# The output stage of an attention and max-of-three layer, done on pairs of token tiles by seven block products

## Chip, cores and metric

The kernel runs on one core of a Trainium2 chip. The metric is the device time of one execution in microseconds (us), lower is better.

## The reference

Attention with a learned bias of relative position, and then a layer that takes the maximum of three products, over 2304 tokens of width 512:

```python
scores = scale * q @ k.T + bias                    # 4 x 8 heads, 576 x 576, head width 64
attn   = exp(scores - max) / (sum + 1e-9)
x      = (attn @ v)                                # rearranged to 2304 x 512
h      = max(max(x @ w1, x @ w2), x @ w3)          # w1, w2, w3: 512 x 768
out    = h @ w_out                                 # w_out: 768 x 512, out 2304 x 512
```

The change touches the last line, and the order in which the line above it is worked out.

## The kernel before, in words

A float32 product is done in three TensorE passes: each operand is split into a high part (a cast to the rounded type float32r, on ScalarE) and a low part (operand minus high part, on VectorE or GpSimd), and a product is high x high + high x low + low x high.

**Attention** runs in 72 steps of 9 per pair of heads and batches (`Attention.step`, L382). Beside it, a stream of small jobs (`first`, L904, drawn by `w0.go`) converts the weights from 64-bit words to float32: per 128 x 512 block one ScalarE operation and four VectorE ones (`convert`, L515). For the sets 3 and 2 of w1..w3 GpSimd also makes four sums of blocks (`sum_w`, L554), and both go to DRAM (`w_d`). The six blocks of w_out are converted in the same stream and stored in `wo_d`. A step draws one VectorE job, or two where the step's number in its nine is 1, 3 or 5 (L977).

**The max-of-three stage** (`moe`, L566) has nine sets of weights: three blocks of 256 columns of h, times the three matrices. h is laid out transposed, with tokens along the columns: three blocks x of 384 columns, each for both halves t of the tokens (1152 each). Set 0 is done plainly (`plain`). The other eight, times three x, are 24 groups (`group`, L592): a Strassen-Winograd scheme with seven products p1 to p7 of 128 x 384, each 6 matmuls of 384 columns, out of four blocks of x (b11, b12, b21, b22) and four sums (t1 to t4). Before, every product has a PSUM bank of its own (8 banks, used in turn); p1 and p5 are copied out by ScalarE (m1, m5), the others are added to them by VectorE, GpSimd makes one add of 768 columns (L614), and the results are put into `ht` by a maximum (two VectorE operations of 768 columns, L623 and L624). After the third set of a column block `store` (L630) writes h to DRAM (`h_d`).

The order is written out by hand: `at(n, k, job)` hangs a job on slot k of group n, and `slot()`, called between products, first takes one entry of the list `after` (the maxima and the stores) and then the jobs of that slot. So preparation of x, of weights and the loads of w_out (L779 to L788) and of h (L817 to L823) stand between products in the queues of ScalarE, VectorE, GpSimd and SyncE, and each queue works in order.

**The output stage** (L840 to L861) goes over 18 tiles of 128 tokens. A tile of h (128 x 768) is loaded from `h_d`, cast by ScalarE (L812) and its low part made by VectorE (L815, through L470); then 18 matmuls of 512 columns: six blocks of 128 of the inner dimension, three passes. ScalarE copies the bank out (L860), SyncE stores it. The last tile is done in two halves of 256 columns. Tile k+1 is prepared, and tile k+5 loaded, before the matmuls of tile k are issued.

Of the kernel before, what the change touches and what calls it, by code (L numbers as in the profile page):

```python
# [19 lines left out]
def kernel(  # L20
# [44 lines left out]
    wo_d = dram.tile([DFF, DM], F32, name="wo_d")  # L65
    w_d = dram.tile([2, 2, 128, 1024], F32, name="w_d")
# [448 lines left out]
    def convert(pool, w, out, name):  # L515
# [13 lines left out]
        nc.vector.scalar_tensor_tensor(out=out, in0=high, scalar=signm, in1=t,  # L529
                                       op0=ALU.bitwise_and, op1=ALU.bitwise_or)  # L530
# [35 lines left out]
    def moe(pool, wpool, x0, xa, xb, raw, sr):  # L566
        ht = pool.tile([128, NX, 5, TW], F32, name="ht", bufs=1)
# [4 lines left out]
        def terms(o, w, xn, r, first, last):  # L572
            hi, lo = w
            h, l = xn
            for j in range(2):
                c = slice(r + 128 * j, r + 128 * j + 128)
                nc.tensor.matmul(o, lhsT=hi[:, c], rhs=h[:, j], start=first and j == 0, stop=False)  # L577
                nc.tensor.matmul(o, lhsT=hi[:, c], rhs=l[:, j], start=False, stop=False)  # L578
                nc.tensor.matmul(o, lhsT=lo[:, c], rhs=h[:, j], start=False, stop=last and j == 1)  # L579

        def plain(x, slot):
            for t in range(2):
                for b in range(2):
                    o = bank(f"c{b}{t}_{x}")[:, 0:TW]
                    for d in range(2):
                        n = (("b11", "b12"), ("b21", "b22"))[d][t]
                        terms(o, wf[0], xs[x][n], 256 * (2 * d + b), d == 0, d == 1)
                        if d:
                            nc.scalar.copy(ht[:, x, 3 * b + t], o)
                        slot()  # L590

        def group(s, x, slot):  # L592
            fp, i = divmod(s, 3)
            acc = ht[:, x]
            q = pool.tile([128, 5, TW], F32, tag="q", bufs=1, name=f"q{s}_{x}") if i else acc
            c21, c22, u, c11, c12 = (q[:, n] for n in range(5))
            m1, m5 = (pool.tile([128, TW], F32, tag="m", bufs=2, name=f"m{n}_{s}_{x}") for n in "15")
            mp = pool.tile([128, 2, TW], F32, tag="mp", bufs=2, name=f"mp{s}_{x}")

            def made(p):  # L600
                o = bank(f"{p}_{s}_{x}")[:, 0:TW]
                w, n = PRODUCTS[p]
                terms(o, wf[s], xs[x][n], 256 * w, True, True)
                return o

            nc.scalar.copy(m1, made("p1"))  # L606
            slot()
            nc.scalar.copy(m5, made("p5"))
            slot()
            arith(v, mp[:, 1], made("p6"), m1, ALU.add)  # L610
            slot()
            arith(v, mp[:, 0], made("p7"), mp[:, 1], ALU.add)
            both = bass.AP(tensor=m5.tensor, offset=m5.offset, ap=[list(m5.ap[0]), [0, 2], [1, TW]])
            g.tensor_tensor(out=q[:, 1:3], in0=mp, in1=both, op=ALU.add)  # L614
            slot()
            arith(v, c11, made("p2"), m1, ALU.add)
            slot()
            arith(v, c21, made("p4"), mp[:, 0], ALU.add)
            slot()
            arith(v, c12, made("p3"), u, ALU.add)  # L620
            slot()
            if i:
                after.append(lambda: arith(v, acc[:, 0:2], acc[:, 0:2], q[:, 0:2], ALU.max))  # L623
                after.append(lambda: arith(v, acc[:, 3:5], acc[:, 3:5], q[:, 3:5], ALU.max))  # L624
            if i == 2:
                after.append(lambda: store(fp, x))
# [3 lines left out]
        def store(fp, x):  # L630
            r = slice(TW * x, TW * x + TW)
            for h in range(2):
                nc.sync.dma_start(out=hd[:, 2 * fp + h, :, r], in_=ht[:, x, 3 * h:3 * h + 2])
# [121 lines left out]
        wor = {}  # L755

        def load_wo(f):
            if f % 2 == 0:
                p, tag = ((wpool, "wr1"), (pool, "wr0"), (wpool, "ws"))[f // 2]
                wor["t"] = p.tile([128, 1024], F32, tag=tag, bufs=1, name=f"wor{f}")  # L760
            wor[f] = wor["t"][:, 512 * (f % 2):512 * (f % 2) + 512]
            nc.sync.dma_start(out=wor[f], in_=wo_d[128 * f:128 * f + 128])

        def raise_wo(f):
            if f == 0:
                for c in "hl":
                    wor[c] = pool.tile([128, 1536], F32R, tag=f"w{c}1", bufs=1, name=f"wo{c}")
            if f < 3:
                wo[f] = tuple(wor[c][:, 512 * f:512 * f + 512] for c in "hl")
            else:  # L770
                wo[f] = tuple(xa.tile([128, 512], F32R, tag=f"f0_{2 * (f - 3) + k}", bufs=1, name=f"wo{c}{f}")
                              for k, c in enumerate("hl"))
            nc.scalar.copy(wo[f][0], wor[f])

        def lower_wo(f, k):
            r = slice(256 * k, 256 * k + 256)
            arith(g, wo[f][1][:, r], wor[f][:, r], wo[f][0][:, r])

        for f in range(KFF):  # L779
            at(23, 0 + (f >= 2) + (f >= 4), F(load_wo, f))  # L780
        n = 3 * NSET - 3
        for f, (up, lows) in enumerate((((n, 0), ((n, 1), (n, 1))), ((n, 3), ((n, 4), (n, 4))),
                                        ((n, 4), ((n, 5), (n, 5))),
                                        ((n + 1, 0), ((n + 1, 1), (n + 1, 1))), ((n + 1, 4), ((n + 1, 5), (n + 1, 5))),
                                        ((n + 2, 0), ((n + 2, 1), (n + 2, 1))))):
            at(*up, F(raise_wo, f))
            for k, where in enumerate(lows):
                at(*where, F(lower_wo, f, k))  # L788

        NK = NT // 128  # L790
        per = TW // 128
        hins = {}
        hs = {}

        def home(k, j, dtype):
            name = f"{('hin', 'hh', 'hl')[j]}{k}"
            if k < 2:
                p, tag = xa, (("f0_6", "f0_7", "r0_0"), ("r0_1", "r0_2", "r0_3"))[k][j]
            else:
                p, tag = xb, f"f1_{3 * ((k - 2) % 3) + j}"  # L800
            return p.tile([128, KFF, 128], dtype, tag=tag, bufs=1, name=name)

        def load_h(k):
            q, c = divmod(k, per)
            x, t = divmod(q, 2)
            hins[k] = home(k, 0, F32)
            c0 = TW * x + 128 * c
            nc.sync.dma_start(out=hins[k], in_=hd[:, :, t, c0:c0 + 128])

        def split_hi(k):  # L810
            hs[k] = (home(k, 1, F32R), home(k, 2, F32R))
            nc.scalar.copy(hs[k][0], hins[k])  # L812

        def split_lo(k):
            arith(v, hs[k][1], hins.pop(k), hs[k][0])  # L815

        n = 3 * NSET - 2  # L817
        at(n, 2, F(load_h, 0))
        at(n, 3, F(load_h, 1))
        at(n + 1, 2, F(load_h, 2), F(split_hi, 0))  # L820
        at(n + 1, 3, F(load_h, 3))
        at(n + 1, 4, F(split_lo, 0))
        at(n + 1, 4, F(load_h, 4))  # L823

        order = [(s, x) for s in range(NSET) for x in range(NX)]
        for n, (s, x) in enumerate(order):
            step = [0]

            def slot():
                for f in after[:1]:  # L830
                    after.pop(0)()
                for f in jobs.pop((n, step[0]), ()):
                    f()
                step[0] += 1

            (plain(x, slot) if s == 0 else group(s, x, slot))
        for f in after:
            f()
        assert not jobs, jobs.keys()
        for k in range(NK):  # L840
            if k + 1 < NK:
                split_hi(k + 1)
                split_lo(k + 1)
            if k + 5 < NK:
                load_h(k + 5)
            hh, hl = hs.pop(k)
            x, t = divmod(k // per, 2)
            t0 = HT * t + TW * x + 128 * (k % per)
            ot = xb.tile([128, DM], F32, tag=f"f2_{k % 4}", bufs=1, name=f"ot{k}")
            parts = 1 if k + 1 < NK else 2  # L850
            for y in range(parts):
                r = slice(y * DM // parts, (y + 1) * DM // parts)
                po = bank(f"o{k}_{y}")[:, 0:DM // parts]
                for f in range(KFF):
                    woh, wol = wo[f]
                    nc.tensor.matmul(po, lhsT=hh[:, f], rhs=woh[:, r], start=(f == 0), stop=False)  # L856
                    nc.tensor.matmul(po, lhsT=hh[:, f], rhs=wol[:, r], start=False, stop=False)  # L857
                for f in range(KFF):
# [186 lines left out]
```

## Time and profile before

| | |
|---|---|
| median of three runs | 587.67 us (587.26 to 588.5) |
| the profiled execution | 587.77 us, of which the span is 586.0 us |
| TensorE busy | 575.4 us, 98% |
| VectorE, ScalarE, GpSimd busy | 76%, 59%, 56% |
| TensorE clock granted | 1.0 in all 40 slices |
| stages of the span | to 306.6 attention, to 331.7 set 0, to 506.9 the 24 groups, to 582.4 the output |

The share of busy time is an average over these four stages, and TensorE is at the top in each. What matters is therefore how long TensorE's instructions in a stage take, and which waits would come to lie between them.

### The profile page before, as it was taken

The page shows a single profiled execution, that of the slowest core. Times are in us where ns is not written, and L with a number is a line of the kernel's source. Part 1 is how long each engine was busy: PE and PEld are TensorE (multiplying, and loading weights), DVE is VectorE, ACT ScalarE, POOL GpSimd, SP SyncE. Part 2 cuts the span into 40 slices and gives each one's busy share as a digit, 9 for nine tenths or more (in the row PEclk, how much of TensorE's full clock was granted, in tenths as well). Part 3 has the DMA queues.
Part 4 walks back from the last instruction along what each step waited for, and adds up shares of the span by engine and source line. Part 5 has one row for each costly group of instructions (what it writes and reads, how often), then busy time and mean ns, then how long its engine had stood idle before and what let it go on. Part 6 is the DMA issues. An engine that isn't in the chain of part 4 may idle for free.

```text
span 586.0 us, 12150 instructions
## 1 busy us (share of the span) xinstructions
PE 575.4 (98%) x4368; PEld 459.6 (78%) x4368; DVE 444.7 (76%) x923; ACT 343.0 (59%) x790; POOL 325.3 (56%) x312
## 2 busy tenths in 40 slices
PE   8999999999999999999999999999999999999997
PEld 4456766666676667676659999999999999988886
DVE  7996779798889999788749899997999566722221
ACT  7996897888888878898746633222212213223231
POOL 1866676876857686776630076686776767400000
PEclk9999999999999999999999999999999999999999
DMA  5898705672684349320001412422123121845442
GB/s 164 240 350 288 254 22 159 219 197 88 196 288 129 105 114 309 107 57 22 22 1 37 141 29 69 158 91 73 36 91 109 36 73 55 242 137 173 141 152 72
DMA packets 70381, 76.85 MB, mean 131 GB/s; under 512 B 22832, under 2 KB 50864, under 8 KB 70320
## 3 DMA queue, kind: packets, MB, share of 16 engines
q1 hardware_dynamic: 70176, 75.77, 41.3%
q8 instruction: 35, 0.57, 0.4%
q10 hardware_dynamic: 144, 0.29, 0.2%
q14 instruction: 26, 0.21, 0.1%
HBM read 49.69 MB, written 26.36 MB: 130 GB/s over the span
## 4 chain that ended last, share of the span: by engine, by line
PE 89%; ACT 5%; DVE 3%; issue 2%; DMA 1%; POOL 0%; DVEq 0%; ACTq 0%
PE pv L359 14%; PE tp L324 11%; PE p L577 10%; PE p L578 10%; PE p L579 10%; PE s L263 10%; PE o L856 4%; PE o L859 4%; PE o L857 4%; PE bp L135 3%; PE s L256 2%; PE c L577 1%; PE c L579 1%; PE c L578 1%; ACT hid L117 1%
## 5 line engine op out<-in xcount | busy, mean ns | idle before, releaser
L298 POOL TENSOR_SCALAR e<-e,rc 128x576 f32<-128x576 f32 x144 | 112.3, 793 | 69.2 <-DVE rc L295 48.9
L286 ACT ACTIVATE e<-sn,nm 128x576 f32<-128x576 f32 x144 | 111.3, 774 | 33.1 <-DVE nm L273 32.1
L273 DVE CUSTOM_DVE_ANT_0 sn<-s,bias 128x576 f32<-128x576 f32 x144 | 103.1, 753 | 21.4 <-PE s L263 17.1
L324 PEld LDWEIGHTS tp<-ident,e 128*128 128x128 f32 x576 | 61.6, 141 | 33.2 <-issue 22.5
L324 PE MATMUL tp<-ident,e 128*128 128x128 f32 x576 | 78.8, 280 | 2.0 <-DVE et L407 1.8
L359 PE MATMUL pv<-et,vt 128*64 128x320 f32 (+1 forms) x496 | 75.3, 419 | 0.1
L606 ACT COPY m<-p 128x384 f32<-128x384 f32 x24 | 11.5, 480 | 94.0 <-PE p L579 52.9
L407 DVE COPY et<-tp 128x512 f32<-128x512 f32 (+1 forms) x80 | 49.6, 629 | 21.0 <-PE tp L324 20.7
L470 DVE TENSOR_TENSOR hl<-hin,hh 128x768 fp32r<-128x768 f32 x18 | 18.1, 1008 | 50.2 <-ACT hh L812 50.2
L614 POOL TENSOR_TENSOR q<-mp,m 128x768 f32<-128x768 f32 x18 | 33.8, 1880 | 36.0 <-DVE mp L470 36.0
L359 PEld LDWEIGHTS pv<-et,vt 128*64 128x64 f32 x496 | 30.8, 136 | 25.2 <-issue 11.1
L263 PE MATMUL s<-kh,qh 64*128 64x288 f32 x256 | 48.5, 344 | 1.2 <-ACT bs L155 0.9
L230 POOL TENSOR_TENSOR kl<-kr,kh 128x576 fp32r<-128x576 f32 x16 | 41.1, 2569 | 15.0 <-ACT kh L227 14.6
L470 DVE TENSOR_TENSOR ht<-ht,q 128x768 f32<-128x768 f32 x36 | 45.8, 1310 | 0.0
L470 POOL TENSOR_TENSOR wl<-wr,wh 128x256 fp32r<-128x256 f32 x25 | 23.6, 955 | 38.5 <-ACT wh L647 38.5
L404 ACT COPY et<-tp 128x512 f32<-128x512 f32 (+1 forms) x72 | 39.5, 548 | 7.9 <-PE tp L324 4.8
L860 ACT COPY ot<-o 128x512 f32<-128x512 f32 (+1 forms) x19 | 10.7, 564 | 56.3 <-PE o L859 56.3
L856 PE MATMUL o<-woh,hh 128*128 128x512 f32 (+1 forms) x114 | 43.4, 385 | 0.0
L135 PE MATMUL bp<-hid,w2s 128*32 128x79 f32 (+51 forms) x640 | 41.0, 393 | 2.2 <-DVE hid L114 1.6
L857 PE MATMUL o<-wol,hh 128*128 128x512 f32 (+1 forms) x114 | 43.0, 381 | 0.0
L263 PE MATMUL s<-kl,qh 64*128 64x288 f32 x256 | 41.0, 295 | 0.0
L114 DVE TENSOR_SCALAR hid<-sm,bp 128x528 f32<-128x528 f32 (+17 forms) x108 | 40.3, 450 | 0.0
(177 smaller groups left out, 1502.2 us busy)
## 6 DMA issues: line engine op xcount, KB each, us to landing
bias_d<-bs SPq DMA_DIRECT2D x36, 295.5 KB, 5.6
bias<-bias_d SPq DMA_DIRECT2D x16, 576.0 KB, 6.4
w<-in_moe_w_dram SPq DMA_DIRECT2D x36, 256.0 KB, 3.3
h_d<-ht SPq DMA_DIRECT2D x18, 384.0 KB, 2.7
hin<-h_d SPq DMA_DIRECT2D x18, 384.0 KB, 3.9
qr<-in_qd_dram SPq DMA_DIRECT2D x16, 288.0 KB, 5.3
kr<-in_kd_dram SPq DMA_DIRECT2D x16, 288.0 KB, 5.1
out_dram<-ot SPq DMA_DIRECT2D x17, 256.0 KB, 4.0
```

The costliest lines, as they stand in the source:

```text
L263: nc.tensor.matmul(ss[h][:, x, 0:HALF], lhsT=u[q][p, 128 * t:128 * t + 128], rhs=u[k][p, cols], start=(j == 0), stop=(j == 2))
L273: nc.vector.tensor_tensor_reduce(out=sn.rearrange("p (a b) -> p a b", a=2), in0=st["s"][h][:, :, 0:HALF], in1=bt.rearrange("p (a b) -> p a ...
L286: nc.scalar.activation(st["e"][:, S * h:S * h + S], sn, ACTF.Exp, scale=-1.0, bias=nm, accum_out=st["sm"][:, h:h + 1])
L298: nc.gpsimd.tensor_scalar(out=e, in0=e, scalar1=rc[:, h:h + 1], scalar2=1.0, op0=ALU.mult, op1=ALU.mult)
L324: nc.tensor.transpose(tp[:, 128 * c:128 * c + 128], e2[:, k0:k0 + 128], ident)
L359: nc.tensor.matmul(pv[p], lhsT=w, rhs=x, start=(c == 0), stop=(c == NTQ))
L470: eng.tensor_tensor(out=out, in0=f(a), in1=f(b), op=op)
L577: nc.tensor.matmul(o, lhsT=hi[:, c], rhs=h[:, j], start=first and j == 0, stop=False)
L578: nc.tensor.matmul(o, lhsT=hi[:, c], rhs=l[:, j], start=False, stop=False)
L579: nc.tensor.matmul(o, lhsT=lo[:, c], rhs=h[:, j], start=False, stop=last and j == 1)
L856: nc.tensor.matmul(po, lhsT=hh[:, f], rhs=woh[:, r], start=(f == 0), stop=False)
L857: nc.tensor.matmul(po, lhsT=hh[:, f], rhs=wol[:, r], start=False, stop=False)
```

## The change

Three parts.

1. *The output stage* takes two tiles of 128 tokens at once, one of each half of the tokens, as a product of 2 x 2 blocks: h by token half and by half of the inner dimension (384), w_out by the same and by half of its columns (256). Seven products with K = 384 and 256 columns replace eight: 9 matmuls each, 63 for a pair, 9 pairs. The sums of blocks of w_out are made during attention and read back (`load_wo`, `raise_wo`, `lower_wo`); those of h are made per pair (`h_sum`), followed by casts (`h_high`) and low parts (`h_low`) of the tiles A (two blocks), B (one), C (t1, t3) and D (t2, t4).
2. *Stages in one bank.* In groups and pairs p6, p7 and p4 go on accumulating on p1's bank, and p3 on p5's; ScalarE copies the bank's content out between (u2, u3). GpSimd's add of 768 columns is gone, and the maximum of the other three blocks is one operation of 1152 columns. The order is p5, p6, p2, p7, p1 of the next group, p4, p3. Slots come before the products. The last two pairs are interleaved.
3. *Attention's stream* converts w_out in blocks like the other weights and makes their sums beside the next conversion (`pend`); a step draws two VectorE jobs only at 1 and 3 of its nine.

```diff
-    wo_d = dram.tile([DFF, DM], F32, name="wo_d")
-    w_d = dram.tile([2, 2, 128, 1024], F32, name="w_d")
+    w_d = dram.tile([2 + KFF // 2, 2, 128, 1024], F32, name="w_d")
...
+            def made(p, on=None):
+                o[p] = o[on] if on else bank(f"{p}_{s}_{x}")[:, 0:TW]
                 w, n = PRODUCTS[p]
+                terms(o[p], wf[s], xs[x][n], 256 * w, not on, True, bool(on))
+                return o[p]
+
+            def p1():
+                o["m1"] = keep("m1", 2)
+                nc.scalar.copy(o["m1"], made("p1"))
+            def p5():
+                made("p5")
+                o["q"] = pool.tile([128, 3, TW], F32, tag="q", bufs=1, name=f"q{s}_{x}") if i else acc[:, 1:4]
+            def p6():
+                o["u2"] = keep("u2", 2)
+                nc.scalar.copy(o["u2"], made("p6", "p1"))
+            def p2():
+                arith(v, o["q"][:, 1], made("p2"), o["m1"], ALU.add)
+            def p7():
+                u3 = keep("u3", 1)
+                nc.scalar.copy(u3, made("p7", "p1"))
+                arith(v, o["q"][:, 0], o["p5"], u3, ALU.add)
+            def p4():
+                if i:
+                    arith(v, acc[:, 0], acc[:, 0], made("p4", "p1"), ALU.max)
+                else:
+                    nc.scalar.copy(acc[:, 0], made("p4", "p1"))
+            def p3():
+                arith(v, o["q"][:, 2], made("p3", "p5"), o["u2"], ALU.add)
+                if i:
+                    after.append(lambda: arith(v, acc[:, 1:4], acc[:, 1:4], o["q"], ALU.max))
+                if i == 2:
+                    after.append(lambda: store(fp, x))
...
+        for k, p in enumerate(USE):
+            at(n - 1, k, F(load_wo, p))
+        for p, up, low, eng in (("p1", (n, 0), (n, 2), v), ("p5", (n, 2), (n, 4), v), ("p6", (n + 1, 0), (n + 1, 1), g),
+                                ("p2", (n + 1, 2), (n + 1, 3), g), ("p7", (n + 1, 4), (n + 1, 5), v),
+                                ("p4", (n + 2, 0), (n + 2, 1), g), ("p3", (n + 2, 4), (n + 2, 4), g)):
+            at(*up, F(raise_wo, p))
+            at(*low, F(lower_wo, p, eng))
...
+        n = 3 * NSET
+        for m in range(NP):
+            at(*((n - 2, 3) if m == 0 else (n - 1, 0) if m == 1 else (n + m - 2, 0)), F(load_h, m))
+            w = n + m - 1
+            if m:
+                at(w, 0, F(h_sum, m, "t1", "t3"), F(h_high, m, "A"))
+                at(w, 2, F(h_high, m, "C"), F(h_sum, m, "t2", "t4"))
+            else:
+                at(w - 1, 6, lambda m=m: h_sum(m, "t3", "t1", "t2", "t4", eng=g))
+                at(w, 0, F(h_high, m, "A"))
+                at(w, 3, F(h_high, m, "C"))
+            at(w, 1, F(h_low, m, "A"))
+            at(w, 3, F(h_low, m, "C"))
+            at(w, 4, F(h_high, m, "B"))
+            at(w, 5, F(h_low, m, "B"))
+            at(w, 6, F(h_high, m, "D"), F(h_low, m, "D"))
...
+                for c in range(3):
+                    k, r = slice(128 * c, 128 * c + 128), slice(256 * c, 256 * c + 256)
+                    nc.tensor.matmul(o[p], lhsT=hi[:, k], rhs=wh[:, r], start=not on and c == 0, stop=False, **skip)
+                    nc.tensor.matmul(o[p], lhsT=hi[:, k], rhs=wl[:, r], start=False, stop=False, **skip)
+                    nc.tensor.matmul(o[p], lhsT=lo[:, k], rhs=wh[:, r], start=False, stop=c == 2, **skip)
...
+        groups = [group(s, x) for s in range(1, NSET) for x in range(NX)] + [out_pair(m) for m in range(NP)]
+        groups[0][0]()
+        for n, (_, p5, p6, p2, p7, p4, p3) in enumerate(groups[:-2]):
+            now[:] = [NX + n, 0]
+            for f in (p5, p6, p2, p7, groups[n + 1][0], p4, p3):
+                slot()
+                f()
+        (_, a5, a6, a2, a7, a4, a3), (b1, b5, b6, b2, b7, b4, b3) = groups[-2:]
+        now[:] = [NX + len(groups) - 2, 0]
+        for f in (a5, a6, a2, a7, b1, a4, b6, a3, b7, b5, b4, b2, b3):
+            slot()
+            f()
...
+                for token in convert(wpool, ahead.pop(0), out, name):
+                    yield token
+                    if token == "vector" and pend:
+                        pend.pop(0)()
...
+            parked = [(f"{s}", s - PARK[1]) for s in PARK] + [(f"o{i}", 2 + i) for i in range(KFF // 2)]
+            for name, k in parked:
+                made, half = block(name)
                 for d in range(2):
+                    yield from conv(lambda: half(d), f"{name}_{d}")
+                nc.sync.dma_start(out=w_d[k, 0], in_=made[0])
+                pend.extend(sums(made[0], name, k))
...
-                more += [w0] * (2 if n % NS in (1, 3, 5) else 1)
+                more += [w0] * (2 if n % NS in (1, 3) else 1)
```

In a pair the functions p1 to p3 are as in a group, with 256 columns, no maximum, and p4 copied out by ScalarE; the low parts of h stand on VectorE, the sums of pair 0 on GpSimd. A token tile is stored whole after p4 (first half of the tokens) and after p3 (second half), and in halves for the last pair.

## Rows read from the trace of the kernel before

**Rows 1.** Busy time by stage: stretch, length, busy us (instructions) of each engine, clock, DMA

```profile
306.56:331.65 25.09, 25.09 (x146) 25.09 (x145) 22.00 (x26) 17.15 (x28) 0.00 (x0) 1.00 0.11 26
331.65:506.85 175.20, 175.20 (x1010) 175.20 (x1009) 145.79 (x199) 47.90 (x84) 122.32 (x105) 1.00 0.27 91
506.85:582.42 75.57, 75.57 (x343) 61.71 (x342) 19.32 (x22) 22.08 (x34) 0.00 (x0) 1.00 0.48 149
582.42:586.00 3.58, 0.00 (x1) 0.00 (x0) 0.00 (x0) 0.37 (x1) 0.00 (x0) 1.00 0.12 39
```

**Rows 2.** Timeline, last two token tiles: start, duration (us), engine, line, operation

```profile
573.82 0.40 PE L856 MATMUL o<-woh,hh 128*128 128x512 f32 x1
...
578.02 0.28 PE L856 MATMUL o<-woh,hh 128*128 128x256 f32 x1
...
580.14 0.28 PE L856 MATMUL o<-woh,hh 128*128 128x256 f32 x1
```

**Rows 3.** Groups of ScalarE by shape, 306 to 586 us: busy us, mean ns, idle before

```profile
L812 ACT CAST hh<-hin 128x768 fp32r<-128x768 f32 x18 | 15.1, 838 | 0.2 <-DMA hin<-h_d 0.2
L608 ACT COPY m<-p 128x384 f32<-128x384 f32 x24 | 11.6, 482 | 4.1 <-PE p L579 4.1
...
L860 ACT COPY ot<-o 128x256 f32<-128x256 f32 x2 | 0.7, 372 | 3.3 <-PE o L859 3.3
```

**Rows 4.** Groups of VectorE by shape, 306.5 to 512 us

```profile
L470 DVE TENSOR_TENSOR ht<-ht,q 128x768 f32<-128x768 f32 x36 | 45.8, 1310 | 0.0
...
L470 DVE TENSOR_TENSOR q<-p,mp 128x384 f32<-128x384 f32 x18 | 9.9, 548 | 2.4 <-PE p L579 2.4
...
L470 DVE TENSOR_TENSOR t<-xb,xb 128x768 f32<-128x768 f32 x4 | 3.8, 952 | 0.0
...
L470 DVE TENSOR_TENSOR hl<-hin,hh 128x768 fp32r<-128x768 f32 x2 | 2.8, 1414 | 0.0
```

**Rows 5.** Timeline of VectorE: one 256-wide copy out of PSUM, two operations back to back

```profile
307.04 0.42 DVE L378 COPY xb<-pvlast 128x256 f32<-128x256 f32 x1
...
318.81 0.95 DVE L470 TENSOR_TENSOR t1l<-t,t1h 128x768 fp32r<-128x768 f32 x1
319.68 0.95 DVE L470 TENSOR_TENSOR t<-xb,xb 128x768 f32<-128x768 f32 x1
```

**Rows 6.** Groups of GpSimd by shape, 300 to 512 us

```profile
L614 POOL TENSOR_TENSOR q<-mp,m 128x768 f32<-128x768 f32 x18 | 33.8, 1880 | 36.0 <-DVE mp L470 36.0
...
L470 POOL TENSOR_TENSOR ws<-wr 128x256 f32<-128x256 f32 x10 | 8.7, 873 | 0.4
```

**Rows 7.** Timeline, groups 25 and 26: the maxima, the stores and loads of h

```profile
492.25 0.33 PE L577 MATMUL p<-b11h,wh 128*128 128x384 f32 x1
...
493.00 2.52 DVE L470 TENSOR_TENSOR ht<-ht,q 128x768 f32<-128x768 f32 x2
...
494.13 1.93 SPq L633 DMA_DIRECT2D h_d<-ht  x2
...
498.42 0.96 SPq L808 DMA_DIRECT2D hin<-h_d  x2
...
503.21 0.83 ACT L812 CAST hh<-hin 128x768 fp32r<-128x768 f32 x1 [0.17 <-DMA hin<-h_d]
```

**Rows 8.** Timeline, attention near 187 us: two conversion operations and TensorE's wait

```profile
185.49 1.42 DVE L521 TENSOR_SCALAR wao<-wao 128x512 f32<-128x512 f32 x1
186.95 1.52 DVE L523 TENSOR_SCALAR wao<-wao 128x512 uint32<-128x512 uint32 x1
...
189.19 1.09 PE L324 MATMUL tp<-ident,e 128*128 128x128 f32 x8 [0.67 <-DVE et L407]
```

**Rows 9.** DMA issues of h: count, KB each, median us to landing

```profile
h_d<-ht SPq DMA_DIRECT2D x18, 384.0 KB, 2.7
hin<-h_d SPq DMA_DIRECT2D x18, 384.0 KB, 3.9
```

More of the change, by code (lines that the diff above doesn't have):

```diff
@@ L566, in moe @@
     def moe(pool, wpool, x0, xa, xb, raw, sr):
[L567 removed]
+        ht = pool.tile([128, NX, 4, TW], F32, name="ht", bufs=1)
         hd = h_d.rearrange("(f p) (t n) -> p f t n", p=128, t=2)
@@ L570, in moe, with terms @@
         v, g = nc.vector, nc.gpsimd
-        def terms(o, w, xn, r, first, last):
+        def terms(o, w, xn, r, first, last, again=False):
             hi, lo = w
@@ L588, in plain, with group @@
                         if d:
-                            nc.scalar.copy(ht[:, x, 3 * b + t], o)
+                            nc.scalar.copy(ht[:, x, 2 * b + t], o)
                         slot()
-        def group(s, x, slot):
+        def group(s, x):
             fp, i = divmod(s, 3)
             acc = ht[:, x]
[L595 to L601, printed above, removed]
-                w, n = PRODUCTS[p]
[L603 to L626, printed above, removed]
@@ L754, in moe @@
         wo = {}
[L755 to L769, printed above, removed]
+        wst = {}
@@ L810, in split_hi @@
[L810 to L837, printed above, removed]
-            f()
[L839 to L858, printed above, removed]
-                    nc.tensor.matmul(po, lhsT=hl[:, f], rhs=wo[f][0][:, r], start=False, stop=(f == KFF - 1))
-                nc.scalar.copy(ot[:, r], po)
-                nc.sync.dma_start(out=out[t0:t0 + 128, r], in_=ot[:, r])
@@ new lines, in moe, with h_high @@
+        HELD = dict(A=("b11", "b21"), B=("b22",), C=("t1", "t3"), D=("t2", "t4"))
+        def h_high(m, c):
+            u, k = hb[m], "ABCD".index(c)
+            parts = []
+            for j in range(2):
+                t = place(m, f"f{k + 4 * j}", F32R, f"{c}{'hl'[j]}")
+                parts.append(t[:, 0] if c == "B" else t)
+            for n, name in enumerate(HELD[c]):
+                u["x" + name] = tuple(t if c == "B" else t[:, n] for t in parts)
+            u["x" + c] = parts
+            nc.scalar.copy(parts[0], u[c])
@@ L912, in conv, with sums, piece @@
                     ahead.append(fetch(wpool, *todo.pop(0)))
-                yield from convert(wpool, ahead.pop(0), out.bitcast(U32), name)
+                for token in convert(wpool, ahead.pop(0), out, name):
+                    yield token
+                    if token == "vector" and pend:
+                        pend.pop(0)()
+            def sums(raw, name, k=None):
+                got = {}
+                def piece(n):
+                    if n == 0:
+                        got["sr"] = sum_tile(wpool, name)
+                        got["gen"] = sum_w(raw, got["sr"])
+                        next(got["gen"])
+                    next(got["gen"], None)
+                    if n == 3 and k is not None:
+                        nc.sync.dma_start(out=w_d[k, 1], in_=got["sr"])
+                    return got["sr"]
+                return [lambda n=n: piece(n) for n in range(4)]
@@ L942, in first @@
-            raw = raw_tile(wpool, 1)
+                pend.extend(lambda k=k, raw=raw: arith(nc.gpsimd, part(lo, k), part(raw, k), part(hi, k))
+                            for k in range(2 * d, 2 * d + 2))
+            made, half = block("1")
             for d in range(2):
-                yield from conv(raw[:, 512 * d:512 * d + 512], f"1_{d}")
-            sr = sum_tile(wpool, 1)
-            yield from sum_w(raw, sr)
-            last.update(raw=raw, sr=sr)
+                yield from conv(lambda: half(d), f"1_{d}")
@@ L949 @@
+            for f in sums(made[0], "1"):
+                yield "vector"
+                sr = f()
+            last.update(raw=made[0], sr=sr)
         w0 = Stream(first())
```

186 lines of the change are left out of this document (132 added, 54 removed).

## Prediction

> **What bounds the kernel now.** I first cut the span at the ends of its stages [rows 1]. After the attention come 25.09 us of set 0, 175.20 us of the 24 product groups and 75.57 us of the output stage; in each of the three TensorE is busy for the whole stretch, at a granted clock of 1.00 (the level of 2.4 GHz), with every other engine below it. So time is saved where TensorE issues less work, and lost where a new wait reaches TensorE. After the last matmul 3.58 us follow, the last copy and the last store. The second view is the timeline of TensorE in the last two token tiles [rows 2]: one tile of 18 matmuls of 512 columns takes 578.02 - 573.82 = 4.20 us, 0.233 us for each matmul. The last tile is cut in halves, and there 18 matmuls of 256 columns start within 580.14 - 578.02 = 2.12 us, 0.1178 us for each. That is the very shape that the change uses everywhere, with new weights in front of each matmul.
>
> **The sums and times.** The profiled execution took 587.77 us (span 586.0), 0.1 us over the median of 587.67. About 0.2%, 1.2 us, is what a measurement can tell from no change.
>
> **Matmuls of the output stage.** Before: 18 x 4.20 = 75.6 us. After: 9 pairs x 7 products x 9 matmuls = 567 matmuls x 0.1178 = 66.8 us, 7.42 us a pair and 1.06 us a product. Change: -8.8 us. The Trainium skill (TensorE: Matmul & The Clock Gate, "Wait — 56ns, not 53.3ns?") gives the time from one warm matmul to the next as N / 2.4 GHz + 2.5 ns; by it, an estimate, 324 x 0.216 = 69.9 us would become 567 x 0.109 = 61.9 us, 8.0 us less. The rows here are 8% above that rule at both widths, and I use them.
>
> **Matmuls of the groups.** The 24 groups keep 42 matmuls of 384 columns each (7.30 us a group), in another order. What is new is that p6, p7 and p4 go on in p1's bank and p3 in p5's. So TensorE waits for the ScalarE copies u2 (before p7) and u3 (before p4) and for VectorE's p5 + u3 (before p3). A product lasts 1.04 us. u2 and u3 cost 0.48 us each [rows 3] while another product runs, which leaves 0.5 us. p5 + u3 is done 0.48 + 0.55 us after p7 [rows 3, 4], and two products (2.08 us) lie between: 1.0 us left. VectorE has less to do per group: four 384-wide operations of 0.55 us and one maximum over 1152, in place of five and two maxima over 768 (1.31 us each); GpSimd's 768-wide add of 1.88 us [rows 6] is gone. I take 0 for these 24 groups; the bounds are 0 and 0.25 us a group, 6 us, for late copies. Below 0 nothing is likely, since TensorE is never idle there.
>
> **Preparation of the pairs, in the steady state.** Per pair ScalarE casts 3 x 0.84 + 0.48 and copies 4 x 0.37 us out of PSUM [rows 3], 4.5 us of 7.42. VectorE makes four 384-wide sums (0.55), three 768-wide low parts (0.95), one of 384 and three 256-wide operations out of PSUM (0.42, from the copy of this width) [rows 4, 5]: 6.9 us by durations. Back to back they start 0.08 us sooner than they last (318.81 to 319.68 is 0.87 [rows 5]), so about 6.0. It fits, so the order decides. Two chains end at TensorE. First, the low part of D (t2, t4) for p6: it is queued on ScalarE behind the copy of p4, so 0.37 + 0.84 + 0.95 = 2.16 us after p4; TensorE gets there after p3, p5 and the two matmuls that need only the high part, 2.36 us. 0.2 us is left. Second, from the low part of D to p5 + u3, VectorE does p3's add, t1, t3, low A, t2, t4, p2's add, low C and then it: 0.33 + 0.46 + 0.46 + 0.87 + 0.46 + 0.55 + 0.33 + 0.87 + 0.42 = 4.75 us, against five products, 5.30. 0.4 us is left. I take 0 a pair; the bounds are 0 and 0.6 us for each of seven pairs. The loads are issued a whole pair ahead and land in 3.9 us [rows 9]: hidden. The bytes stay the same, 768 KB in and 512 KB out a pair.
>
> **The last two pairs.** Their products are interleaved, and pair 8's p6 comes straight after pair 7's p4. The chain of 2.16 us is then covered by two matmuls only: a wait of 2.16 - 0.24 = 1.9 us. I see nothing that hides it. Bounds 1.0 (if the cast slips ahead of the copy) and 2.5.
>
> **The passage into the output stage.** Pair 0 needs all of h for x = 0, which group 24 ends. Before, group 25 starts at 492.25, the two maxima run from 493.00 to 495.5, the stores are issued from 494.13, and the loads that wait for them go out at 498.42 and hold ScalarE until 503.21 [rows 7]. After, p1 of group 25 comes ahead of group 24's last two products, so p3 ends at 493.3, its add at 493.85, and the one maximum over 1152 (1.5 times 0.87 to 1.31) at 495.2 to 495.8. Both stores wait for it, so the loads start near 498.9 and land near 503.0 and 503.7. The cast of A is queued on ScalarE at the head of group 26, whose p5 starts at 500.6. It ends at 503.84, so u2 ends at 504.3 where p7 wanted to start at 503.7: 0.6 us. The sums of pair 0 run on GpSimd, 0.94 us each (half of 1.88 [rows 6]): t3 and t1 are done at 505.6, the cast of C at 506.4, and u3, queued behind it, at 506.9; p4 wanted 506.4: 0.5 us more. In pair 0 VectorE must also make the last maximum (1.3 us), while GpSimd still runs two 768-wide low parts of w_out. A 768-wide VectorE operation took 1.41 us here against 0.95 in such company [rows 4]. So p5 + u3 of pair 0 comes 6.2 + 0.5 to 1.0 us after low D (510.3), p3 wants to start at 515.35: a wait of 1.2 to 2.1, I take 1.6. The sum is 2.7 us; bounds 0 (h lands a microsecond sooner, and all of it falls away) and 4.5.
>
> On the last of these the Trainium skill (SBUF — State Buffer, the shared port pair of VectorE and GpSimd) says that an operation of either with two SBUF inputs blocks the other's until it ends. By it alone pair 0 could wait for two whole operations of 1.88 us. The row shows half a microsecond for one operation on average, which I use.
>
> **Attention.** The w_out blocks now get their sums ahead of time: 12 more GpSimd operations of 256 columns, 0.87 us each [rows 6], and no VectorE work more. They are issued beside the conversion of the next block, and since raw has one buffer, the last conversion operation of each next block waits on VectorE for the fourth sum; queued behind it are the reciprocal and the copy of the transposes that TensorE waits for. This happens five times. On the other side the steps with two such operations at y = 5 go: in one of them 1.42 and 1.52 us on VectorE end in a TensorE wait of 0.67 us [rows 8]. I take 0, with bounds -0.7 (that wait gone) and +2.0 (five waits of 0.4 us).
>
> The tail stays: one add of 0.42 us in place of the copy of 0.37 us, then a half store as before.
>
> **Sum.** -8.8 + 0 + 0 + 1.9 + 2.7 + 0 = -4.2 us: 587.7 - 4.2 = 583.5 us.
>
> **Rivals.**
> - *The passage costs nothing.* h lands before the cast of A is due, and pair 0 catches up. For it: the loads are due within 0.6 us of the need. Against: the maximum of 1152 stands ahead of both stores. Time 587.7 - 8.8 + 1.9 = 580.8.
> - *VectorE bounds every pair.* The chain from low D to p5 + u3 has 0.4 us left in 5.3; if each of its nine operations starts 0.1 us later than I count, 0.5 us a pair is lost. For it: 6.9 of 7.42 us by durations. Against: back-to-back starts show overlap. Time 583.5 + 7 x 0.5 = 587.0.
> - *Slower: the waits inside one bank.* In the 24 groups u2 and u3 stand on ScalarE behind casts of 0.84 us and behind what those wait for, and TensorE stops where it had other banks to go on in. Price: from 0.22 us a group (5.3 us) the kernel is slower than before by over 0.2%; at 0.25 us it takes 589.5. For it: a cast of 0.84 us ahead of a copy is longer than the 0.5 us left. Against: 47.90 us of 175.20 busy [rows 1], and the casts are queued where a product of cover is left. The Trainium skill (PSUM — Partial Sum Buffer, "PSUM bank collisions raise a hardware error") asks that accesses of two engines to one bank be ordered by semaphores; that is why these waits exist, and no row shows what one costs.
> - *The stage is shorter but attention pays.* The five waits delay the transposes by 2 us: 585.5.
>
> **How the numbers follow.** Forecast 0.50 (582 to 585), faster. The free passage 0.13, faster. VectorE in every pair 0.20: between 0.4 and 0.6 us a pair it ends within 1.2 us of the time before, so 0.11 of it counts as the same, 0.06 as faster, 0.03 as slower. Waits inside a bank 0.12: 0.11 slower, 0.01 the same. Attention 0.05: 0.03 faster, 0.02 the same. Faster 0.72, same 0.14, slower 0.14. The range leaves out the waits inside a bank and the fastest end of the free passage: 580.5 to 588.0.
>
> **What would show it.** In the changed profile the stage from the first 256-wide matmul of pair 0 to the last should last about 72 us, with 567 matmuls starting 0.118 us apart. The waits of TensorE should name ScalarE's cast of C and VectorE's low part at the last p6 (1.9 us) and near 503 to 517. The 24 groups should still take 7.30 us each. The forecast is wrong if TensorE is idle a little in every group (waits for u2, u3), if it waits in every pair for p5 + u3, or if the 256-wide matmuls start more than 0.125 us apart.

## The result: slower, and where the time went

The changed kernel takes 595.17 us, the median of four runs (592.87 to 597.21), against 588.09 us for the kernel before beside it: a ratio of 1.0115, 95% interval 1.0083 to 1.0147. The forecast was 583.5 us, faster. The profiled execution took 596.17 us with a span of 594.4 us, 8.4 us over the span before.

First the stages, as in [rows 1] (stretch, length, busy us and instructions of PE, PEld, DVE, ACT, POOL, then clock and DMA):

```profile
312.33:337.39 25.06, 25.06 (x145) 25.06 (x145) 21.99 (x26) 17.15 (x28) 0.00 (x0) 1.00 0.04 9
337.39:513.91 176.52, 173.83 (x998) 173.19 (x997) 107.14 (x154) 62.15 (x112) 65.95 (x72) 1.00 0.28 93
513.91:591.11 77.20, 71.65 (x580) 69.52 (x579) 57.66 (x97) 37.42 (x73) 8.56 (x6) 0.98 0.49 152
591.11:594.40 3.29, 0.00 (x0) 0.00 (x0) 0.42 (x1) 0.00 (x0) 0.00 (x0) 0.89 0.24 80
...
351.36:497.48 146.12, 146.12 (x842) 146.12 (x841) 85.91 (x130) 48.38 (x89) 54.87 (x62) 1.00 0.25 84
```

Two things stand out. Set 0 begins at 312.33 in place of 306.56, so 5.8 us are lost before any stage that the forecast gave a price other than 0 (1.0 of them in the start, see below). And TensorE, busy in every microsecond of [rows 1], is not so in the second and third line: 2.7 and 5.6 us are idle. The last line is 20 product groups that nothing disturbs: 7.306 us each, against 7.30 before.

The timeline of TensorE names the halts. In brackets stand the idle time ahead of an instruction and what ended it:

```profile
204.51 1.09 PE L323 MATMUL tp<-ident,e 128*128 128x128 f32 x4 [3.39 <-DVE et L406]
...
344.96 0.44 PE L577 MATMUL p<-t4h,wh 128*128 128x384 f32 x1 [1.15 <-ACT u L624]
...
512.75 0.44 PE L577 MATMUL p<-t3h,wh 128*128 128x384 f32 x1 [1.54 <-ACT u L617]
...
516.45 0.45 PE L577 MATMUL p<-t4h,wh 128*128 128x384 f32 x1 [1.32 <-ACT u L624]
...
520.89 0.39 PE L894 MATMUL p_o<-wohp,Dl 128*128 128x256 f32 x1 [0.77 <-DVE Dl L469]
...
525.62 0.38 PE L894 MATMUL p_o<-woh,Al 128*128 128x256 f32 x1 [1.28 <-DVE Al L469]
...
528.22 0.38 PE L892 MATMUL p_o<-wohp,Bh 128*128 128x256 f32 x1 [0.50 <-DVE ot L469]
...
581.17 0.39 PE L892 MATMUL p_o<-wohp,Dh 128*128 128x256 f32 x1 [1.19 <-ACT Dh L855]
...
582.16 0.39 PE L894 MATMUL p_o<-wohp,Dl 128*128 128x256 f32 x1 [0.49 <-DVE Dl L469]
```

Five halts from 512 to 529 make 5.41 us, the last pair 1.68, one in group 4 1.15, and one in attention 3.39. ("Group 4" is the first of the 24 product groups, on which `at(3, ...)` hangs its jobs; groups 24 to 26 are named by the kernel's own count, which starts at 0.) Between 530 and 580 there is none: the five pairs from the third to the seventh take 36.73 us, 7.35 us a pair.

**The halt in attention**, on GpSimd and VectorE:

```profile
197.49 1.83 POOL L469 TENSOR_TENSOR b11l<-xb,b11h 128x768 fp32r<-128x768 f32 x1
199.26 0.74 POOL L469 TENSOR_TENSOR wso<-wr 128x256 f32<-128x256 f32 x1
199.99 1.46 POOL L297 TENSOR_SCALAR e<-e,rc 128x576 f32<-128x576 f32 x2
201.42 0.72 POOL L469 TENSOR_TENSOR wso<-wr,wso 128x256 f32<-128x256 f32 x1
...
202.17 0.75 DVE L528 SCALAR_TENSOR_TENSOR wr<-w64o,signm,wao 128x512 uint32<-128x512 uint32 x1 [3.88 <-POOL wso L469]
202.84 0.95 DVE L469 TENSOR_TENSOR t<-xb,xb 128x768 f32<-128x768 f32 x1
...
203.78 0.67 DVE L406 COPY et<-tp 128x512 f32<-128x512 f32 x1
```

The fourth sum of a w_out block ends at 202.14, behind a low part, the third sum and two multiplications of the softmax. VectorE's conversion of the next block writes over the raw block that this sum reads, so VectorE stands still for 3.88 us; the sum t and the copy of the transposes are queued behind, and TensorE waits for that copy.

**The passage**, on all engines:

```profile
500.68 1.84 POOL L469 TENSOR_TENSOR wolp<-wop,wohp 128x768 fp32r<-128x768 f32 x1 [20.60 <-ACT wohp L793]
501.41 2.33 DVE L469 TENSOR_TENSOR ht<-ht,q 128x1152 f32<-128x1152 f32 x1
...
503.77 1.18 SPq L647 DMA_DIRECT2D h_d<-ht  x2
...
507.67 2.78 SPq L824 DMA_DIRECT2D hin<-h_d  x4
508.70 1.36 DVE L469 TENSOR_TENSOR ht<-ht,q 128x1152 f32<-128x1152 f32 x1
...
511.49 0.83 ACT L855 CAST Ah<-hin 128x768 fp32r<-128x768 f32 x1 [4.17 <-DMA hin<-h_d]
512.94 1.24 POOL L469 TENSOR_TENSOR C<-hin 128x384 f32<-128x384 f32 x1 [6.89 <-DMA hin<-h_d]
514.14 1.00 POOL L469 TENSOR_TENSOR C<-hin,hin 128x384 f32<-128x384 f32 x1
...
515.18 0.83 ACT L855 CAST Ch<-C 128x768 fp32r<-128x768 f32 x1 [2.48 <-POOL C L469]
...
517.85 4.69 POOL L469 TENSOR_TENSOR wolp<-wop,wohp 128x768 fp32r<-128x768 f32 x2
...
518.79 2.04 DVE L469 TENSOR_TENSOR Dl<-D,Dh 128x768 fp32r<-128x768 f32 x1
...
521.34 2.42 DVE L469 TENSOR_TENSOR ht<-ht,q 128x1152 f32<-128x1152 f32 x1
```

It is the chain of [rows 7] with the maximum, the stores, the loads and the cast in their places. Each cast waits for h or for C, and the copies u2 and u3 that TensorE needs stand behind these casts on ScalarE.

**The clock.** Windows of two microseconds (columns as above), first in attention, then in the last pair:

```profile
202.00:204.00 2.00, 0.00 (x0) 0.00 (x0) 1.83 (x4) 0.85 (x2) 0.14 (x1) 1.00 0.50 195
204.00:206.00 2.00, 1.49 (x7) 1.16 (x8) 2.00 (x6) 1.44 (x4) 1.46 (x2) 0.64 1.02 290
206.00:208.00 2.00, 2.00 (x14) 1.61 (x16) 1.28 (x5) 1.80 (x8) 1.47 (x2) 0.50 0.89 313
...
582.00:584.00 2.00, 1.84 (x13) 1.84 (x14) 0.10 (x1) 0.37 (x1) 0.00 (x0) 0.86 0.00 0
584.00:586.00 2.00, 2.00 (x11) 2.00 (x11) 0.42 (x1) 0.00 (x0) 0.00 (x0) 0.50 0.00 0
586.00:588.00 2.00, 2.00 (x15) 2.00 (x15) 0.00 (x0) 0.37 (x1) 0.00 (x0) 0.78 0.35 131
```

Behind both halts the granted clock falls to 0.50, the level of 1.2 GHz. From 584 to 586 ten matmuls start, 0.213 us apart; in the same two microseconds of the same kernel run again (below), at 1.00, seventeen do, 0.113 us apart. [rows 1] have 1.00 in every stretch.

Two marks cut the span into parts that can be compared between executions. **Stretch A** goes from the first matmul of the first mixed step of attention (s from kr and qr: 57.19 us before, 58.20 after) to the first matmul of set 0; **stretch B** from there to the start of the last matmul. A grew from 249.37 to 254.13 us (+4.8), B from 275.6 to 278.5 (+2.9). The start took 1.0 us longer, and the tail is 0.3 us shorter. The start is no part of the change: in the profiles below its mark lies between 56.80 and 62.07 us. Where the same kernel was run again B grew by 1.05 us only and A by 5.4, so most of what was lost lies in attention, and in the rest of the span the halts ate up all that the matmuls had saved.

### The profile page after: what moved, and what is told of

It reads as the page before. It is cut to its first block, busy times and chain, and to the rows that moved or that the text cites. A ratio compares the mean times of both kernels' runs of the same rounds, so it can differ in the third digit from the quotient of the medians.

```text
span 594.4 us, 12566 instructions
## 1 busy us (share of the span) xinstructions
PE 572.1 (96%) x4593; PEld 466.9 (79%) x4593; DVE 445.0 (75%) x955; ACT 372.8 (63%) x856; POOL 286.1 (48%) x296
## 4 chain that ended last, share of the span: by engine, by line
PE 81%; ACT 5%; DVE 5%; DMA 4%; POOL 3%; issue 2%; SPq 0%; DVEq 0%; POOLq 0%
PE pv L358 13%; PE tp L323 11%; PE p L577 9%; PE p L579 9%; PE p L578 9%; PE s L262 9%; PE p_o L894 4%; PE p_o L892 3%; PE p_o L893 3%; PE bp L134 3%; PE s L255 2%; PE c L577 1%; PE c L579 1%; PE c L578 1%; ACT hid L116 1%
## 5 line engine op out<-in xcount | busy, mean ns | idle before, releaser
L617 ACT COPY u<-p 128x384 f32<-128x384 f32 x24 | 11.5, 479 | 57.8 <-PE p L579 57.6
L262 PE MATMUL s<-kh,ql 64*128 64x288 f32 x256 | 39.8, 293 | 0.2 <-POOL ql L229 0.2
L134 PEld LDWEIGHTS bp<-hid,w2s 128*32 128x32 f32 x640 | 20.7, 110 | 22.8 <-issue 13.3
L262 PEld LDWEIGHTS s<-kh,qh 64*128 64x128 f32 x256 | 26.5, 186 | 13.0 <-issue 6.0
L469 DVE TENSOR_TENSOR q<-p,u 128x384 f32<-128x384 f32 x36 | 20.0, 555 | 19.7 <-ACT u L624 16.2
L469 POOL TENSOR_TENSOR wl<-ws,wh 128x256 fp32r<-128x256 f32 x28 | 27.0, 993 | 15.0 <-ACT wh L663 15.0
L624 ACT COPY u<-p 128x384 f32<-128x384 f32 x24 | 11.5, 479 | 31.2 <-PE p L579 31.2
```

The costliest lines, as they stand in the source:

```text
L134: nc.tensor.matmul(bp[32 * c:32 * c + 32, o:o + w], lhsT=w2s, rhs=src, start=True, stop=True)
L262: nc.tensor.matmul(ss[h][:, x, 0:HALF], lhsT=u[q][p, 128 * t:128 * t + 128], rhs=u[k][p, cols], start=(j == 0), stop=(j == 2))
L469: eng.tensor_tensor(out=out, in0=f(a), in1=f(b), op=op)
```

## The experiments

All kernels are made from the changed one. "Ratio" is to the kernel before, measured beside them; the changed kernel's is 1.0115.

| kernel | median us | ratio (95%) | A us | B us |
|---|---|---|---|---|
| changed | 595.17 | 1.0115 (1.0083 to 1.0147) | 254.13 | 278.50 |
| the same again, one run | 594.16 | | 254.76 | 276.63 |
| sums two at a time | 591.56 | 1.0069 (1.0046 to 1.0091) | 250.62 | 276.37 |
| D first in the last pair | 592.87 | 1.0093 (1.0071 to 1.0115) | 255.22 | 274.73 |
| halt filled | 594.16 | 1.0107 (1.0094 to 1.0120) | 255.34 | 276.35 |
| four edits | 586.6 | 0.9975 (0.9960 to 0.9989) | 248.87 | 273.49 |
| passage reordered | 590.55 | 1.0035 (1.0015 to 1.0056) | 254.01 | 272.71 |
| four edits, second passage | 583.8 | 0.9921 (0.9894 to 0.9947) | 250.53 | 269.62 |
| no sums of w_out | 588.89 | 1.0006 (0.9988 to 1.0023) | 248.96 | 276.48 |
| t2's cast later | 594.13 | 1.0117 (1.0094 to 1.0140) | 255.28 | 276.12 |

**Attention: the sums left out.**

```diff
-                pend.extend(sums(made[0], name, k))
+                if name[0] == "o":
+                    nc.sync.dma_start(out=w_d[k, 1], in_=made[0])
+                else:
+                    pend.extend(sums(made[0], name, k))
```

> The twelve GpSimd sums of w_out blocks in the attention stage are left out (the raw block is stored in their place, so the output stage computes with other weights). Theory (they alone delay attention): from the marker of the first step to the first set-0 matmul 249.4 us as before the change, in place of 254.1, and no halt of TensorE of 3.4 us near 204; median near 590.5. Rival (the removed conversion steps or another part of the edit delays attention): this stretch stays above 252 us and the median above 593.

A is 248.96 us, the halt near 204 us is gone, and the clock stays at 1.00. The twelve sums and what they drag along cost 5.2 us of A in the first profile of the changed kernel, and 5.0 to 6.4 in the six profiles that have the halt of 3.4 us. What else the edit moved in attention costs nothing in sum. The median, 588.89, is 1.6 us under the expectation; by the ratios the sums cost 0.0109, which is 6.4 us.

**Attention: the sums kept, issued in another place.**

```diff
-                    if token == "vector" and pend:
-                        pend.pop(0)()
+                    for _ in range(2 if token == "vector" else 0):
+                        if pend:
+                            pend.pop(0)()
```

> Edit: in attention the four GpSimd sums of a block are issued two at a time beside the first two conversion operations of the next block, so the fourth is done well ahead of the last conversion operation, which overwrites the block; nothing is added or left out. Theory (the wait): in the changed kernel VectorE stood 3.9 us before that operation, TensorE 3.4 us, and the granted clock fell to 0.50 behind it; without the wait no VectorE wait for GpSimd over 1 us is left there, the clock stays at 1.00, and set 0 starts near 307 to 308 us in place of 312.3; time about 591. Rival (the work): the twelve more GpSimd sums slow attention whatever their order; then set 0 still starts near 311 to 312 and the time stays near 595.

A is 250.62: 3.5 of the 5.2 us are back with the same work on GpSimd. By the ratios, each known to 0.002 or 0.003, it is less, 0.0046 of 0.0109, and the execution that was profiled was the fastest of six. VectorE's wait for the fourth sum shrank to 0.74 us, and what is left of TensorE's halt comes after an operation of 2.30 us beside b11l (1.84 us on GpSimd), like the 2.43 us in front of the wait of 0.91 us before the change. First the kernel of this run:

```profile
196.62 2.30 DVE L528 SCALAR_TENSOR_TENSOR wr<-w64o,signm,wao 128x512 uint32<-128x512 uint32 x1 [0.74 <-POOL wso L469]
...
200.51 0.66 PE L323 MATMUL tp<-ident,e 128*128 128x128 f32 x4 [1.83 <-DVE et L406]
```

Then the kernel before:

```profile
193.42 2.43 DVE L529 SCALAR_TENSOR_TENSOR wso<-w64o,signm,wao 128x512 uint32<-128x512 uint32 x1
...
196.66 1.06 PE L324 MATMUL tp<-ident,e 128*128 128x128 f32 x8 [0.91 <-DVE et L407]
```

The clock did not stay at 1.00, as the theory had it: from 201.7 to 205.1 us it was 0.50. What this costs can be read from the two kernels with four edits below, whose attention is the same. In the second of them A is 250.53 with such a fall; in the first it is 248.87, the same as without the sums, and the clock stayed at 1.00 although the halt of 1.84 us is there:

```profile
202.00:204.00 2.00, 1.20 (x8) 0.82 (x8) 2.00 (x6) 1.44 (x3) 2.00 (x4) 1.00 0.71 188
204.00:206.00 2.00, 2.00 (x19) 1.35 (x21) 2.00 (x7) 1.97 (x10) 1.96 (x3) 1.00 0.93 266
```

So in the traces the price was the place of the sums in the queue, with the fall of the clock behind the halt; the added work by itself shows no cost. By the times, in which the clock can fall more or less often from one execution to the next, the split between the two is not settled.

**The last pair: D ahead of B.**

```diff
+            else:
+                at(w, 4, F(h_high, m, "D"), F(h_low, m, "D"))
+                at(w, 7, F(h_high, m, "B"))
+                at(w, 8, F(h_low, m, "B"))
```

> Edit: for the last pair alone the high and low part of D are made before those of B, ahead of the copies that p6 of the last pair stood behind. Theory: TensorE's wait before p6 of the last pair (1.19 + 0.49 us) falls to about 0.4 us, and the granted clock, which fell to 0.50 about 2.5 us behind that wait, stays at 1.00; TensorE ends about 3 us sooner, time about 592 to 593. Rival: the clock falls at the end whether or not TensorE waits there; then 1.3 us are won, about 594.

Of the two halts one of 0.21 us is left. The last 126 matmuls, two pairs, start within 14.87 us. In the changed kernel's first profile they take 18.36 us, and 16.62 where the clock stayed up, as with the sums two at a time: the halts cost 1.75 us, and the clock 1.74 where it fell. The ratio, 1.0093, is not clear of that of the changed kernel; the gain is shown in the traces alone.

```profile
585.10 0.39 PE L899 MATMUL p_o<-wohp,Dl 128*128 128x256 f32 x1 [0.21 <-DVE Dl L469]
```

**The last pair: the halt filled with matmuls that nobody reads.**

```diff
+            if f is b6:
+                spare = bank("spare")[:, 0:256]
+                for k in range(15):
+                    nc.tensor.matmul(spare, lhsT=wo["p1"][0][:, 0:128], rhs=wo["p1"][0][:, 0:256],
+                                     start=k == 0, stop=k == 14)
```

> Edit: 15 matmuls of 256 columns whose result nobody reads, on a bank of their own, are put in front of p6 of the last pair, where TensorE waited 1.7 us; p6 can start no sooner. Theory (the idle time costs twice, once as a wait and once as a lower clock behind it): the clock stays at 1.00 to the end and TensorE ends about 1.6 us sooner although it does 1.8 us more work; time about 594. Rival (the clock has nothing to do with the idle time): it falls to 0.50 as before, and the time stays at 595 or is a little higher.

B is 276.35 with a clock of 1.00 at the end. That does not bear out the theory: four other kernels with the halts unfilled (sums two at a time, no sums, the passage alone, t2's cast later) kept the clock too. So the changed kernel was run once more.

**The same kernel again.**

> The changed kernel once more, for the granted clock behind the waits of 1.19 and 0.49 us in the last pair. If the clock follows from the wait's length alone it falls to 0.50 there as in the first profile, and the stretch from the first set-0 matmul to the last matmul is 278.5 us; if it does not, the clock stays 1.00 there, as in the three runs with the same waits, and the stretch is 276.4 us.

The halts are there (1.19 and 0.49 us) and the clock stays at 1.00. B is 276.63:

```profile
582.00:584.00 2.00, 2.00 (x18) 2.00 (x19) 0.00 (x0) 0.37 (x1) 0.00 (x0) 1.00 0.00 0
584.00:586.00 2.00, 2.00 (x20) 2.00 (x19) 0.42 (x1) 0.37 (x1) 0.00 (x0) 1.00 0.32 122
```

So the fall at the end belongs to that one execution, one of six with those halts. The fall in attention was there in every profile with the halt of 3.4 us.

**Group 4: the cast of t2 behind the copy.**

```diff
-        at(3, 3, F(b2.sum, "t4"), F(b2.high, "t2"))
-        at(3, 4, F(b2.low, "t2"))
-        at(3, 5, F(b2.high, "t4"))
+        at(3, 3, F(b2.sum, "t4"))
+        at(3, 4, F(b2.high, "t2"))
+        at(3, 5, F(b2.low, "t2"), F(b2.high, "t4"))
```

> Only the cast of t2 in group 4 is issued one slot later, behind the copy u3, and its low part one slot later. Theory (u3 stood behind a cast that had to wait for VectorE's sum t4): the wait of 1.15 us near 345 us goes and no other comes in groups 4 and 5; median 1.1 us lower, about 594. Rival (the low part of t2 is now late for p6 of group 5, or p3's add is): a wait of 0.5 us or more appears in group 5, no gain.

The halt of 1.15 us is gone and none came in its place: from the first matmul of the first product group to the first of the third it takes 12.55 us, in place of 13.94 where the same kernel was run again. That is 1.39 us for a halt of 1.15. All profiles agree: 12.54 to 12.55 us in the three with this edit, 13.94 to 13.97 in the seven without. The median does not show it (1.0117): in that profile three of the five steady pairs took 7.52 us each and two 7.35, and B is only 0.5 us under the same kernel run again beside it. In the trace the gain is plain; in the time it is not shown by this run alone.

**All four, with a first order of the passage** (the sums of pair 0 on VectorE, the maximum of group 26 ahead of t2 and t4):

> Edit: the two edits of the runs above on the sums and on the last pair, and two more: in group 4 the cast of t2 (which waits for a sum) goes behind the copy u3; and in the passage to the output stage group 26 runs as p6, p5, p7, p2, p4, p3 with pair 0's p1 last, pair 0's sums go to VectorE, its casts stand behind the copies u2 and u3, and the last maximum is made after p5 + u3 of pair 0. Theory (the saving of 8.8 us in the output matmuls is there, and is given back in named waits): attention -5, group 4 -1.1, passage -3.5, last pair -3: about 583, under the kernel before. Rival (the rest of the loss is spread over all groups and pairs, as accumulation in one bank): no better than about 589.

It is faster than both, 0.9975, yet short of the expectation. The halts of the passage had moved to C, and behind the first of them the clock fell: it is 0.50 from 514 to 518 us.

```profile
512.32 0.38 PE L900 MATMUL p_o<-woh,Ch 128*128 128x256 f32 x1 [1.82 <-ACT Ch L855]
...
515.25 0.58 PE L902 MATMUL p_o<-woh,Cl 128*128 128x256 f32 x1 [2.43 <-DVE Cl L469]
```

**The passage alone, reordered a second time.**

```diff
-                                 ... ("p3", (n + 2, 4), (n + 2, 4), g)):
+                                 ... ("p3", (n + 2, 0), (n + 2, 1), g)):
...
+            if m == 0:
+                at(w, 2, F(h_sum, m, "t3", "t1"))
+                at(w, 3, F(h_high, m, "A"), F(h_low, m, "A"), F(h_high, m, "C"), F(h_sum, m, "t2", "t4"))
+                at(w, 5, F(h_low, m, "C"), F(h_high, m, "D"))
+                at(w, 6, F(h_low, m, "D"))
+                at(w + 1, 1, F(h_high, m, "B"), F(h_low, m, "B"))
+                continue
...
+            held = now == [3 * NSET - 1, 6] or (now[0] == 3 * NSET and now[1] < 4)
+            for f in () if held else after[:1]:
...
+            if NX + n == 3 * NSET - 1:
+                order = (p6, p5, p7, p2, p4, p3, nxt)
+            elif NX + n == 3 * NSET:
+                order = (p2, p5, p6, p7, nxt, p4, p3)
```

> Only the passage into the output stage is reordered: the last block of w_out is converted one slot group earlier, h of pair 0 gets its sums t3 and t1 on VectorE ahead of the adds of group 26, the casts of A and C go behind the copy u3, the last maximum goes behind pair 0's preparation, and pair 0 starts with p2. Theory (the five waits of 5.4 us in the passage are the order of work behind the landing of h, not its landing): the waits of TensorE from group 26 to pair 1 fall to about 1 us, the stretch from the first set-0 matmul to the last matmul from 278.5 to about 274, the median to about 590.5. Rival (h simply lands too late, so a wait only moves): the waits stay above 4 us and the median stays near 594 to 595.

Two halts are left, 0.75 and 1.00 us in place of 5.4 (and one of 0.12); B is 272.71, 3.9 us under the same kernel run again, and the ratio falls to 1.0035. The order of the work, with the sums of pair 0 on VectorE, was the cause; which of the moves gave how much was not tried. A part stays with the landing of h, as the next kernel shows too.

**All four with this passage.**

> The passage of the run before this one, with the sums of attention two at a time, D ahead of B in the last pair, and the cast of t2 later in group 4. Theory (each named wait is a loss of its own and they add): about 582.5, 4 us under the version with the first reordering of the passage, whose waits for C (1.8 and 2.4 us) and the half clock after them are gone; the granted clock is 1.00 from 204 us to the last matmul. Rival (the passage's waits only move): 586 to 587.

583.8 us, 0.9921: faster than both kernels. The parts add up nearly: by the ratios the sums gave 0.0046, the last pair 0.0022 and the passage 0.0080, and 1.4 us in the trace of group 4 is 0.0024; that makes 0.0172, and the step from 1.0115 to 0.9921 is 0.0194, each ratio being known to 0.002 or 0.003. What is left of the passage is a wait of VectorE for h, which holds up p5 + u3 and so p3 of group 26, and a copy behind the cast of C:

```profile
506.38 0.56 DVE L469 TENSOR_TENSOR C<-hin 128x384 f32<-128x384 f32 x1 [2.11 <-DMA hin<-h_d]
...
507.93 0.44 PE L577 MATMUL p<-b22h,wh 128*128 128x384 f32 x1 [0.82 <-DVE q L469]
...
515.06 0.39 PE L899 MATMUL p_o<-wohp,Ch 128*128 128x256 f32 x1 [0.98 <-ACT u2o L925]
```

The expectation that the clock would be 1.00 from 204 us on did not hold: after a halt of 1.84 us in attention it was 0.50 from 202 to 204 us.

## Why the prediction was wrong, step by step

- **Matmuls of the output stage: right.** 7.35 us a pair, against 7.42 forecast: 75.6 - 9 x 7.35 = 9.4 us saved. The Trainium skill (TensorE: Matmul & The Clock Gate, "Wait — 56ns, not 53.3ns?") gives 109 ns for this width; the trace has 7.35 / 63 = 117 ns, 7% more, and the row of before was the better guide.
- **The 24 groups: right, but for one.** 7.306 us each; the rival of waits inside one bank did not come true as a loss in every group. Its mechanism, a copy u2 or u3 behind a cast that waits, did: in group 4 and twice in the passage, 4.0 us of halts. The halt in group 4 was not in the sum: the cast of t2 waits there for VectorE's t4, and u3 stands behind it. 1.4 us.
- **Steady pairs: right.** No halt; VectorE does not bound them. (5.30 - 4.75 in the working is 0.55 us left, not 0.4; nothing hangs on it.) **The last pair: right**, 1.68 us of halts for 1.9.
- **The passage: mis-sized**, 5.4 us for 2.7, and above the upper bound of 4.5. Three of its terms were small. The maximum took 2.33 us beside GpSimd's low part, not 1.3 to 2.0, and the cast of A began 1.2 us later than forecast, counted from where group 25 starts (497.48 plus two products of the group before: 11.9 us, for 10.75); GpSimd's sums of pair 0 took 1.24 and 1.00 us, not 0.94; and "p5 + u3 late by 1.6" was in truth low D, 2.04 us, and a maximum of 2.42 us which took low A of pair 1 with it.
- **Attention at 0: the step that failed.** The forecast took "five waits of 0.4 us" as the upper end, about half of a sum's duration. The five waits are there, and VectorE stood 2.05, 1.43, 0.07, 3.88 and 1.41 us in them (the first two for sums of w1 to w3, which the edit moved too). What a wait costs here is not the sum's duration but what stands ahead of it on GpSimd: the third and fourth sum go out one per step of the conversion, behind low parts and softmax. Only the wait of 3.88 us held TensorE for long. With its clock it made 4.8 to 5.2 us, and up to 6.4 in the other profiles: more than the 4.2 us that the whole change was to gain, and more than twice the bound of 2.0.
- **Two terms were missing.** A halt cost more than its idle time: 1.39 for 1.15 in group 4. At some 0.2 us for each of the eight halts in B this is an estimate of 1.6 us. And the clock fell behind a halt, 1.74 us at the end of the first profile.

The sum of B by the trace of the first profile: -9.4 (pairs) + 1.15 + 5.41 + 1.68 (halts) + 1.6 (their restarts) + 1.74 (clock) + 0.1 (groups) = +2.3 us, against +2.9 measured; 0.6 us are not assigned.

The prediction weighed the port that VectorE and GpSimd share and took an average of half a microsecond an operation from [rows 4]. The rows of the passage show more: the maximum takes 1.36 us with GpSimd idle (at 508.70) and 2.33 us when it starts 0.73 us after a low part of 1.84 us, which ran on unslowed. What it lost, 0.97 us, is about what was left of that low part, 1.11 us. Low D, which takes 0.95 us otherwise, lost 1.09 in the same way, with 1.23 us left of a low part of 2.17. The Trainium skill (SBUF — State Buffer, "Who interferes with whom") says that when a VectorE instruction with two SBUF inputs meets a GpSimd instruction that reads SBUF, the second to issue waits until the first has ended; the trace agrees within 0.2 us. The trace of the kernel before had it too: the 1.41 us of [rows 4] are the mean of two operations, one that met a GpSimd operation and one that met none.

```profile
504.66 1.85 POOL L614 TENSOR_TENSOR q<-mp,m 128x768 f32<-128x768 f32 x1 [0.97 <-DVE mp L470]
505.44 1.88 DVE L470 TENSOR_TENSOR hl<-hin,hh 128x768 fp32r<-128x768 f32 x1
...
509.92 0.95 DVE L470 TENSOR_TENSOR hl<-hin,hh 128x768 fp32r<-128x768 f32 x1
```

An average over both was the wrong price for an operation that meets another.

## What to carry to other kernels

When work is moved to a stage that TensorE bounds, price each new wait by the queue in front of the instruction that ends it, not by that instruction's duration, and then by everything queued behind the one that waits. Here more than half of the 9 us that the output stage saved was lost to twelve small operations in a stage 300 us earlier; putting nearly the same operations in another order, there and in three other places, turned 1.2% slower into 0.8% faster. A halt should be entered at more than its length.

## What the runs showed of the hardware

- The clock can fall to 0.50 for a few microseconds in or behind a short halt: at 3.4 us of idle in attention in all six profiles that had it (in three of them well before the halt was over), at 1.83 and 1.84 us in two of three (not in the first version of the four edits), at halts of 1.82 and 2.43 us in that version's passage, and behind 1.19 and 0.49 us in one of six. The halts of 1.3 to 1.7 us in the passage were followed by no fall in any of seven profiles. What decides between them stays open. The times roughly follow the clock: the four runs of the changed kernel took 592.87, 594.17, 596.17 and 597.21 us at mean granted clocks of 0.996, 0.994, 0.994 and 0.991.
- A halt of 1.15 us cost 1.39 to 1.43 us. After the halt at 581.17 the second matmul starts 0.22 us after the first, where in the stream it is 0.118.
- The pace of equal matmuls differs between executions and within one: the steady pairs took 7.33 to 7.35 us each in nine profiles; in the one with t2's cast later the first three took 7.52 and the last two 7.35. The same kernel run again beside it had 7.35 throughout, so it is not the chip. The cause stays open.
